# Sliding-window attention with a gated MLP on one core: other queues for the first batch, and folds of two head pairs at once in the second

## The chip, the cores and the metric

The kernel runs on one core of a Trainium2 chip. Its time is the device time of one execution in microseconds. Before the change it is 303.85 us, the median of 3 runs (303.29 to 304.75). The profiled execution took 304.4 us, of which the profile's span covers 302.7; the rest lies around it.

The engines are TensorE (PE; its weight loads are shown as PEld), VectorE (DVE), ScalarE (ACT), GpSimd (POOL) and SyncE (SP). DMA transfers are issued from SP's queue and from POOL's queue. Only the transfers that POOL issues can change the type of what they move (the casting queue).

## The reference

Eight batches of eight heads, 576 positions, 64 values per head. Each query sees itself and the 63 positions before it. The result of the attention, with the heads side by side, goes through an MLP with a gate of its own.

```python
batch, n_heads, seq, head_dim = (8, 8, 576, 64)
n_tokens, d_model, d_ff = (4608, 512, 2048)

scores = scale * np.matmul(q, k.transpose(0, 1, 3, 2))     # scale = 1/8
mask = (rel >= 0) & (rel < window)                         # window = 64
scores = np.where(mask, scores, -1000000000.0)
attn = softmax(scores)
x = np.matmul(attn, v)                # heads side by side: (4608, 512)
h = x @ w_in
g = h * np.clip(h + 3.0, 0.0, 6.0) / 6.0
out = g @ w_out
```

## The kernel before

Everything is computed in bf16 with f32 sums. The heads are taken in four pairs per batch, since a head has 64 values and a tile 128 partitions. The attention of a batch works in blocks of 64 queries: eight blocks per pair with their 128 keys each (64 before, 64 own), and the ninth block of all four pairs together, called "e".

The MLP works on tiles of 512 tokens, nine in all (`NTT`), as if the batches were one long list. For each tile, 16 chunks of the hidden layer are computed by L685 (`s1_part`, `win` against `xT`), gated by ACT (L698) and DVE (L703) into `gT`, and multiplied by `wout` (L724, `s2_part`), 64 matmuls of 512 columns per tile and direction. The attention of batch b+1 is woven into the MLP of tile b.

The order of the instructions of each engine is computed when the kernel is built. A planner (class `Plan`) holds every step with its engine, an assumed duration, what it reads and writes and a priority, and puts the steps in an order by list scheduling. Some steps may go to one of several engines (`copy_op`, `alts`), and the planner picks. The table `LANDED` gives it assumed landing times for the transfers of the first batch. What comes out is a fixed order for each engine; every engine then works through its own list and waits where its next step is not ready. The accumulators in PSUM are two banks `pn` and three double banks (`pb`, two `pa`), handed out by the planner too.

**Batch 0.** q and k must be turned so that the 64 values of a head lie along the partitions. They are loaded with nine neighbouring positions per partition (`A`, [128, 4 pairs, 9, 64]). Pair 0 comes by SP as f32 into `stage` (`load_pair`) and is cast by DVE or ACT (L343); pairs 1 to 3 come by POOL's casting queue, one transfer per pair and tensor (`load_cast`). `fold_pair` turns a pair with 18 TensorE transposes of 64x64 (L490): head h of the pair uses rows and output partitions 64h to 64h+63. One copy (L495, 576 columns) brings the result from PSUM into `F_`. `scores` first adds a far negative number to the masked places with `ident` and `far` (L514) and then multiplies (L529), two heads in turn in the two row halves.

V is wanted twice: as it lies, and shifted by 64 positions, because a block's keys begin at a multiple of 64. In batch 0, V of pairs 0 and 1 comes by SP as f32 into a second `stage` (`load_tok`, four transfers), and `cast_v` casts it straight into both places (L343, pieces on ACT and DVE). V of pairs 2 and 3 comes by the casting queue (`load_vhead`, one transfer per head), and `shift_v` copies it (L433, two copies per pair: 4 blocks and 3 blocks) on POOL, ACT or DVE. `pv_rows` multiplies (L574, columns of TensorE in halves) and normalises on DVE (L584, L585); `turn_x` turns the result (L600) into `xT`.

**Batch 1.** q and k are loaded by two `load_cast` per tensor (pairs 0, 1 and pairs 2, 3) and turned with `fold_pair` again, eight times. V comes by POOL in rows (`load_vrows`), one transfer per block, and `shift_v` copies each pair.

**Batches 2 to 7.** `load_rows` brings q and k as rows by POOL into `nq` and `nk`, and two DMA transposes on SP's queue turn them into `Tq` and `Tk`. A small POOL copy (L801, `hold`) keeps the next transfers back until `Tk` is there; then V and the rows of the following batch are issued.

POOL's queue is one list: transfers are issued in the order of the chain (`then`), each 0.5 to 0.9 us, with POOL's own copies between them where the planner puts them. Eight semaphores are used in turn for POOL's transfers, so a transfer waits until the one eight places earlier has landed.

Of the kernel before, what the change touches and what calls it, by code (L numbers as in the profile page):

```python
# [23 lines left out]
    "SP": (2970, 3660, 6210, 7840, 8150, 10350),  # L24
    "POOL": (4550, 6480, 7920, 9200, 10360, 10930, 11370, 11790, 12210, 12680),
# [187 lines left out]
def kernel(  # L213
# [41 lines left out]
    def wide(op, name):  # L255
        s, k = op.got[name]
        return banks[k][s]
# [10 lines left out]
    NST = 2  # L268
# [17 lines left out]
    def k_cols(b, r, g, j):  # L286
        k0 = max(j - 1, 0) * D
        if b < ROWS_FROM:
            return F_["k"][r, g, k0 : k0 + P]
        return T_["k"][r, g, k0 : k0 + P]  # L290
# [37 lines left out]
    def act(n):  # L328
        return 160 + n / 1.2
# [54 lines left out]
    def load_pair(n, src, b, g, i, x):  # L384
        st = stage[i][:, x * R * D : (x + 1) * R * D]
        dma(P, 106, st, src[b, 2 * g : 2 * g + 2].rearrange("h (p j) d -> (h p) (j d)", j=R), writes=[("stp", n, g)])
        copy_op(R * D, A[n][:, g, :, :].rearrange("p j d -> p (j d)"), st, ("ACT", "DVE"),
                [("stp", n, g)], [("A", n, g)] + st_keys(i, 0, NG, range(KB)), sbuf=True, prio=700)
# [5 lines left out]

    def load_tok(src, b, i, g0, g1, kbs=tuple(range(KB))):
        st = stage[i][:].rearrange("p (k h d) -> p k h d", k=KB, h=H)
        hs = slice(2 * g0, 2 * g1)
        for kb in kbs:
            s0, ss = kb * P, min(P, S - kb * P)
            dma(ss * (g1 - g0) * 2, 18, st[:ss, kb, hs, :],  # L400
                src[b, hs, s0 : s0 + ss, :].rearrange("h s d -> s h d"),
                writes=st_keys(i, g0, g1, (kb,)))

    def load_heads(src, b, i, g):

        st = stage[i][:].rearrange("p (k h d) -> p k h d", k=KB, h=H)
        for h in range(2):
            dma(NE * P, 18, st[:, 0:NE, 2 * g + h, :], src[b, 2 * g + h, 0:MAIN, :].rearrange("(k s) d -> s k d", k=NE),
                writes=st_keys(i, g, g + 1, range(NE), (h,)))
        load_tok(src, b, i, g, g + 1, (NE,))  # L410

    def st_keys(i, g0, g1, kbs, hs=(0, 1)):
        return [("st", i, g, kb, h) for g in range(g0, g1) for kb in kbs for h in hs]
# [25 lines left out]

    def cast_v(i, g0, g1, engines, prio=0, after=(), parts=((0, NE), (NE, NE)), pieces=(0, 1, 2)):  # L440
        st = stage[i][:].rearrange("p (k g h d) -> p k g h d", k=KB, g=NG, h=2)
        gs = slice(g0, g1)
        vv = V[:, :, :, 0 : 3 * D].rearrange("p k g (t d) -> p k g t d", d=D)
        full, odd = parts
        for x, (rows, src, k0, (y, n)) in enumerate((
            (slice(0, P), slice(0, P), 0, full),
            (slice(0, D), slice(D, P), 0, odd),
            (slice(D, P), slice(0, D), 1, odd),
        )):
            if not n or x not in pieces:  # L450
                continue
            blks = range(y, y + n)
            k0 += y % NE
            copy_op(n * (g1 - g0) * P, vv[rows, y : y + n, gs, 0:3:2, :], st[src, k0 : k0 + n, gs, :, :], engines[x],
                    st_keys(i, g0, g1, range(k0, k0 + n)), [("V", g, x, blk) for g in range(g0, g1) for blk in blks],
                    sbuf=True, prio=prio, after=after)
# [9 lines left out]
    def v_block(j):  # L466
        return j // 2 if j % 2 or j == 0 else NE + j // 2 - 1
# [11 lines left out]
    def fold_pair(n, g, b, gate, kinds=("n", "b", "a")):  # L479
# [19 lines left out]
        e = add("DVE", 0, None, reads=[key], writes=[t_key(n, b, g)], alts=alts, stream="copy", prio=(1400 if g == NG - 1 else 700) if b == 0 else 300)  # L499
# [3 lines left out]
    def scores(b, items, gate, stream="att", pr=300, masked=False, kinds=("a",)):  # L503
# [18 lines left out]
        def em():  # L522
            for x, name in zip(items, names):
                to = wide(add_far if masked else op, name)
                for y in range(NG if x == "e" else NM):
                    g, j = (y, NM) if x == "e" else (x, y)
                    for h in range(2):
                        r = slice(h * D, (h + 1) * D)
                        nc.tensor.matmul(to[:, h, y * D : (y + 1) * D], lhsT=k_cols(b, r, g, j),  # L529
                                         rhs=q_cols(b, r, g, j), start=not masked,  # L530
                                         stop=not masked or y == NM - 1)
# [3 lines left out]
        for x, name, key in zip(items, names, keys):  # L535
# [8 lines left out]
            def ex(name=name, n=n, p_=p_):  # L544
                nc.scalar.activation(out=p_[:].rearrange("p j h c -> p h j c"),  # L545
                                     in_=wide(add_far if masked else op, name)[:, :, 0 : n * D].rearrange("p h (j c) -> p h j c", c=D),
                                     func=EXP, scale=scale)
# [61 lines left out]
    def pv(b, x, i, after=(), stream="att", pr=300):  # L609
# [12 lines left out]
        def em():  # L622
            for h in range(2):
                for y in range(n // D):
                    g, blk, p_ = (y, 2 * NE - 1, p9[b % 2]) if end else (x, v_block(y), pT[i])
                    nc.tensor.matmul(wide(op, name)[:, h, y * D : (y + 1) * D], lhsT=V[:, blk, g, h * D : h * D + P],  # L626
                                     rhs=p_[:, y, h, :], start=True, stop=True)
# [205 lines left out]
    NOW, REST = ((0, NE), (NE, NE - 1)), ((0, 0), (2 * NE - 1, 1))  # L833
# [29 lines left out]
    for t in range(NTT):  # L863
# [24 lines left out]
        if b < B:  # L888
            if b == 1:
                gate = (hs[4],)  # L890
                cast_v(iv, 0, 2, (THREE,) * 3, parts=REST, prio=-2500, pieces=(1,))
# [66 lines left out]
```

## Time and profile before

| | |
|---|---|
| median of 3 runs | 303.85 us |
| the profiled execution | 304.4 us |
| its span | 302.7 us |
| TensorE busy | 289.8 us (96%) |
| DVE, ACT, POOL busy | 199.6, 207.5, 127.1 us |
| read from and written to HBM | 36.70 MB, 9.44 MB |
| L724, one matmul of 512 columns, start to start | 0.215 us |
| first matmul of L685 | 17.34 us |
| L685 of tile 1 begins | 55.36 us |

Times inside the span count from its start. A line of a timeline has the start, the duration, the engine, the line of the kernel, the operation, what it writes and reads, how often, and in brackets the idle time before it with what ended it. A line of the chain of waits has the start, the duration and what the end of the program was waiting for in that time; "DMA Ak<-in_k_dram" is the time from the issue of a transfer to its landing. Busy shares of TensorE contain the overlap of matmuls and say little alone: a wait shows as a gap between starts.

### The profile page before, as it was taken

How to read it: one execution, taken by the hardware profiler on the slowest of the kernel's cores; microseconds unless marked ns; L12 is line 12 of the kernel's file. 1: busy time of each engine (PE TensorE's matmuls, PEld its weight loads, DVE VectorE, ACT ScalarE, POOL GpSimd, SP SyncE). 2: the span in 40 equal slices, each digit the busy share in tenths (PEclk: the TensorE clock that was granted, in tenths of full speed). 3: DMA queues.
4: the chain of work that ended last, by engine and by line, in shares of the span. 5: the costliest groups of instructions: out<-in, count | busy, mean ns of one | idle time of the engine just before them, and what ended most of it. 6: DMA issues, size and time to landing. Idle time of an engine off the chain costs nothing.

```text
span 302.7 us, 6789 instructions
## 1 busy us (share of the span) xinstructions
PE 289.8 (96%) x2703; PEld 154.5 (51%) x2749; DVE 199.6 (66%) x326; ACT 207.5 (69%) x323; POOL 127.1 (42%) x178
## 2 busy tenths in 40 slices
PE   7799998999999999999999999999999999999996
PEld 6544554445544454445587554455445544444443
DVE  3659737686578795788777885778678767206700
ACT  4768846678778785878678767877687858217711
POOL 8874769409920990496089229803200000000000
DMA  8999999999998999999999989948900010011011
GB/s 169 194 209 205 205 185 111 109 193 89 166 115 183 99 144 151 177 128 90 204 178 120 135 162 175 128 90 163 141 2 35 36 69 3 35 69 37 0 69 69
DMA packets 137760, 36.65 MB, mean 121 GB/s; under 512 B 126337, under 2 KB 132993, under 8 KB 137729
## 3 DMA queue, kind: packets, MB, share of 16 engines
q0 software_dynamic: 98896, 17.80, 73.0%
q1 hardware_dynamic: 38832, 18.42, 24.7%
q8 instruction: 21, 0.34, 0.5%
q14 instruction: 11, 0.08, 0.1%
HBM read 36.70 MB, written 9.44 MB: 152 GB/s over the span
## 4 chain that ended last, share of the span: by engine, by line
PE 77%; DMA 10%; POOL 6%; issue 4%; DVE 1%; ACT 0%; SPq 0%; POOLq 0%; DVEq 0%
PE pn L724 33%; PE pn L685 15%; PE pa L685 12%; PE pb L685 8%; DMA Ak<-in_k_dram 7%; PE pa L626 4%; POOL nk L366 2%; DMA Tk<-nk 2%; DMA V<-in_v_dram 1%; PE pa L529 1%; POOL V L433 1%; PE pa L724 1%; POOL nq L366 1%; POOL V L366 1%; PE pb L626 1%
## 5 line engine op out<-in xcount | busy, mean ns | idle before, releaser
L724 PE MATMUL pn<-wout,gT 128*128 128x512 bf16 x532 | 125.2, 379 | 2.1 <-issue 1.1
L685 PEld LDWEIGHTS <-win 128*128 128x128 bf16 x640 | 61.9, 98 | 60.8 <-issue 0.3
L724 PEld LDWEIGHTS <-gT 128*128 128x128 bf16 x592 | 54.1, 98 | 57.5
L685 PE MATMUL pn<-xT,win 128*128 128x512 bf16 (+1 forms) x274 | 63.2, 358 | 0.4
L703 DVE SCALAR_TENSOR_TENSOR gT<-t,pn 128x512 bf16<-128x512 bf16 x63 | 43.1, 686 | 11.1 <-ACT t L698 10.9
L698 ACT ACTIVATE t<-pn,half 128x512 bf16<-128x512 f32 x63 | 43.3, 689 | 9.9 <-PE pn L685 9.4
L685 PE MATMUL pa<-xT,win 128*128 128x512 bf16 (+1 forms) x202 | 48.0, 358 | 0.3
L703 DVE SCALAR_TENSOR_TENSOR gT<-t,pa 128x512 bf16<-128x512 bf16 x47 | 32.1, 687 | 23.7 <-ACT t L698 23.4
L366 POOL DMA_DIRECT2D nk<-in_k_dram x60 | 45.9, 812 | 1.2 <-DMA Ak<-in_k_dram 0.7
L698 ACT ACTIVATE t<-pa,half 128x512 bf16<-128x512 f32 x47 | 32.1, 687 | 8.6 <-PE pa L685 8.1
L646 DVE TENSOR_TENSOR xT<-pa,rec 64x512 bf16<-64x512 f32 (+1 forms) x48 | 32.5, 677 | 6.7 <-ACT rec L635 5.7
L685 PE MATMUL pb<-xT,win 128*128 128x512 bf16 (+1 forms) x149 | 35.3, 357 | 0.5 <-issue 0.5
L366 POOL DMA_DIRECT2D V<-in_v_dram x40 | 33.2, 853 | 4.7 <-PE pa L529 1.2
L703 DVE SCALAR_TENSOR_TENSOR gT<-t,pb 128x512 bf16<-128x512 bf16 x34 | 23.3, 687 | 16.3 <-ACT t L698 16.3
L737 ACT COPY osb<-pn 128x512 f32<-128x512 f32 x18 | 10.5, 585 | 33.5 <-PE pn L724 33.5
L632 ACT ACTIVATE rec<-pa 64x512 f32<-64x512 f32 (+1 forms) x48 | 27.9, 582 | 5.2 <-PE pa L626 4.1
L801 POOL COPY scrap<-Tk 128x1 bf16<-128x1 bf16 x6 | 1.1, 188 | 69.5 <-DMA Tk<-nk 69.5
L698 ACT ACTIVATE t<-pb,half 128x512 bf16<-128x512 f32 x34 | 23.4, 689 | 7.7 <-PE pb L685 7.7
L366 POOL DMA_DIRECT2D nq<-in_q_dram x30 | 27.6, 920 | 2.4 <-DMA wout<-in_moe_w_out_dram 1.6
L545 ACT ACTIVATE pT<-pa 128x1024 bf16<-128x1024 f32 x24 | 23.6, 1020 | 0.5 <-PE pa L529 0.5
L626 PEld LDWEIGHTS <-V 128*128 128x128 bf16 x464 | 17.5, 98 | 8.8 <-DVE xT L646 1.5
L554 DVE TENSOR_TENSOR pT<-pT,mask 128x1024 bf16<-128x1024 bf16 x28 | 19.1, 698 | 4.1 <-ACT pT L545 4.0
(88 smaller groups left out, 210.0 us busy)
## 6 DMA issues: line engine op xcount, KB each, us to landing
out_dram<-osb SPq DMA_DIRECT2D x35, 256.0 KB, 2.5
V<-in_v_dram POOLq DMA_DIRECT2D x28, 128.0 KB, 4.3
nq<-in_q_dram POOLq DMA_DIRECT2D x24, 128.0 KB, 4.1
nk<-in_k_dram POOLq DMA_DIRECT2D x48, 64.0 KB, 3.9
wout<-in_moe_w_out_dram POOLq DMA_DIRECT2D x4, 512.0 KB, 14.8
win<-in_moe_w_in_dram POOLq DMA_DIRECT2D x3, 512.0 KB, 9.8
V<-in_v_dram POOLq DMA_DIRECT2D x12, 64.0 KB, 5.6
Aq<-in_q_dram POOLq DMA_DIRECT2D x2, 288.0 KB, 14.0
```

Of the source, the lines that this page charges most:

```text
L366: em = lambda: e.dma_start(out=out_ap, in_=in_ap)
L433: alts = {e: (c, (lambda e=e, rows=rows, src=src, k0=k0, n=n: cpy(e)(out=vv[rows, NE : NE + n, gs, 0:3:2, :], in_=vv[src, k0 : k0 + n, gs, ...
L545: nc.scalar.activation(out=p_[:].rearrange("p j h c -> p h j c"), in_=wide(add_far if masked else op, name)[:, :, 0 : n * D].rearrange("p ...
L554: nc.vector.tensor_tensor(out=pp, in0=pp, in1=mask[:, m0 : m0 + n, :, :].rearrange("p j h c -> p (j h c)"), op=MULT)
L626: nc.tensor.matmul(wide(op, name)[:, h, y * D : (y + 1) * D], lhsT=V[:, blk, g, h * D : h * D + P], rhs=p_[:, y, h, :], start=True, stop=True)
L632: add("ACT", act(n), lambda h=h: nc.scalar.activation(out=rc[rows[h], 0:n], in_=wide(op, name)[rows[1 - h], h, 0:n], func=LN), reads=[key] ...
L646: nc.vector.tensor_tensor(out=o, in0=a, in1=z, op=MULT)
L685: nc.tensor.matmul(bank(op, name)[:, to : to + n], lhsT=win16[:, g, fc * P : (fc + 1) * P], rhs=xT[:, g, o : o + n], start=(g == 0), stop= ...
L698: nc.scalar.activation(out=t1[ti][:], in_=bank(op, name), func=RELU, bias=half[:], scale=1.0 / 6.0)
L703: nc.vector.scalar_tensor_tensor(out=gT[:, fc, :], in0=t1[ti][:], scalar=1.0, in1=bank(op, name), op0=MIN, op1=MULT)
L724: nc.tensor.matmul(bank(op, name)[:, 0:n], lhsT=gT[:, fc, col : col + P], rhs=wout16[:, fc, js], start=(fc == 0), stop=(fc == NFC - 1))
L737: alts = {e: (f(n), (lambda e=e: cpy(e)(out=osb[oi][:, js], in_=bank(op, name)[:, 0:n])), False) for e, f in (("DVE", dve), ("ACT", act))}
```

## The change

There are three parts. The lines L626, L685, L724 and so on are those of the kernel before.

1. Batch 0: SP loads q and k of pairs 0 and 1 as f32 (four big transfers, into the one `stage` that is left). The casting queue loads q and k of pairs 2 and 3 in one transfer each, and V of all four pairs by heads (eight transfers). `load_tok`, `load_heads` and `cast_v` go; `shift_v` now copies all four pairs.
2. Batch 1: `fold_quad` turns two pairs at once: 18 transposes with all 128 rows and 128 columns, pair g in output partitions 64(g mod 2) to 64(g mod 2)+63, and one copy of 1152 columns instead of two of 576. Four such folds take the place of eight. In `F_` of batch 1 the row half is now given by the parity of the pair, not by the head.
3. The scores of batch 1 therefore alternate between two pairs, so that neighbouring matmuls use different row halves; the block "e" is stored in another order, which its exponential and `pv` follow.

The assumed landing times in `LANDED` change with the transfers. In the order that the planner makes of it, batch 1 has five shift copies of V on POOL and three on DVE (before: six and two), and all four copies out of the folds on ACT (before: four on ACT, four on DVE). From tile 1 on the order of all engines is as before.

```diff
 LANDED = {
-    "SP": (2970, 3660, 6210, 7840, 8150, 10350),
-    "POOL": (4550, 6480, 7920, 9200, 10360, 10930, 11370, 11790, 12210, 12680),
+    "SP": (2900, 3700, 5400, 7100),
+    "POOL": (7100, 8900, 9350, 9800, 10250, 10700, 11150, 11600, 12050, 12500),
 }
...
-    NST = 2
+    NST = 1
...
+    QUAD = 1
+
+    def half_rows(b, g, h):
+        x = g % 2 if b == QUAD else h
+        return slice(x * D, (x + 1) * D)
+
-    def q_cols(b, r, g, j):
+    def q_cols(b, g, h, j):
+        r = half_rows(b, g, h)
         if b < ROWS_FROM:
-            return F_["q"][r, g, j * D : (j + 1) * D]
+            return F_["q"][r, g // 2 * 2 + h if b == QUAD else g, j * D : (j + 1) * D]
...
+    def fold_quad(n, y, b, gate):
+
+        name = ("F", n, b, y)
+        key = ("ps", name)
+        gs = (2 * y, 2 * y + 1)
+        op = pe(R * 60, None, [("A", n, g) for g in gs] + ["ident"], [key], "pick", alloc=(name,), kinds=("b", "a"), after=gate, mode="c")
+
+        def flat():
+            return wide(op, name).rearrange("p x c -> p (x c)").bitcast(BF16)
+
+        def em():
+            for j in range(R):
+                for g in gs:
+                    nc.tensor.transpose(out=flat()[(g % 2) * D : (g % 2 + 1) * D, j * P : (j + 1) * P], in_=A[n][:, g, j, :], identity=ident[:])
+
+        op.emit = em
+
+        def ev(eng):
+            cpy(eng)(out=F_[n][:, 2 * y : 2 * y + 2, :].rearrange("d h (p j) -> d h p j", j=R),
+                     in_=flat()[:, 0 : R * P].rearrange("d (j h p) -> d h p j", h=2, p=D))
...
+            if b == QUAD:
+                todo = [t for pair in zip(*([t for t in todo if t[1] % 2 == x] for x in range(2))) for t in pair]
+            for name, g, h, y, j in todo:
+                u, y = (y % 2, y // 2 * 2 + h) if b == QUAD and j == NM else (h, y)
+                nc.tensor.matmul(wide(add_far if masked else op, name)[:, u, y * D : (y + 1) * D], lhsT=k_cols(b, g, h, j),
+                                 rhs=q_cols(b, g, h, j), start=not masked, stop=not masked or y == NM - 1)
...
-    i0, iv = new_stage(), new_stage()
-    load_pair("q", q, 0, 0, i0, 0)
-    load_pair("k", k, 0, 0, i0, 1)
-    load_tok(v, 0, iv, 0, 2, range(NE))
-    then(load_cast("q", q, 0, 1, 2))
-    then(load_cast("k", k, 0, 1, 2, after=chain))
+    i0 = new_stage()
+    for g in range(2):
+        load_pair("q", q, 0, g, i0, 2 * g)
+        load_pair("k", k, 0, g, i0, 2 * g + 1)
+    then(load_cast("q", q, 0, 2, 4))
+    then(load_cast("k", k, 0, 2, 4, after=chain))
     then(add("POOL", 600, lambda: make_identity(nc, ident32), writes=["c32"], after=chain))
-    then(load_cast("q", q, 0, 2, 3, after=chain))
-    then(load_cast("k", k, 0, 2, 3, after=chain))
     then(add("POOL", 900, mask_pool, writes=["m32"], after=chain))
     add("DVE", 550, far_mask, reads=["m32"], writes=["far"], prio=600)
-    then(load_cast("q", q, 0, 3, 4, after=chain))
-    then(load_cast("k", k, 0, 3, 4, after=chain))
-    for g in range(2, NG):
+    for g in range(NG):
         for h in range(2):
             then(load_vhead(0, g, h, chain)).prio = 3000
...
-    for parts in ((0, 2), (NE, 1)), ((2, 2), (NE + 1, 2)):
-        cast_v(iv, 0, 2, (THREE,) * 3, prio=700, parts=parts)
...
-    for g in range(2, NG):
+    for g in range(NG):
         shift_v(g, g + 1, THREE, 700)
...
-                for g in range(NG):
+                for y in range(NG // 2):
                     for n in "qk":
-                        fold_pair(n, g, 1, gate, ("b", "a"))
+                        fold_quad(n, y, 1, gate)
```

More of the change, by code (lines that the diff above doesn't have):

```diff
@@ L438, in shift_v @@
                 stream="copy" if len(engines) > 1 else engines[0])
[L440 to L456, printed above, removed]
     V_PARTS = [(0, blk) for blk in range(NE)] + [(x, NE + blk) for x in (1, 2) for blk in range(NE - 1)]
@@ L522, in em @@
         def em():
+            todo = []
             for x, name in zip(items, names):
-                to = wide(add_far if masked else op, name)
                 for y in range(NG if x == "e" else NM):
                     g, j = (y, NM) if x == "e" else (x, y)
[L527 to L531, printed above, removed]
+                    todo += [(name, g, h, y, j) for h in range(2)]
+            if b == QUAD:
[4 more added lines that the diff above has]
+                                 rhs=q_cols(b, g, h, j), start=not masked, stop=not masked or y == NM - 1)
         op.emit = em
@@ L542, in scores, with ex @@
                 got.append(i)
-            def ex(name=name, n=n, p_=p_):
-                nc.scalar.activation(out=p_[:].rearrange("p j h c -> p h j c"),
+            def ex(name=name, n=n, p_=p_, to="p (x y) h c -> p x (y h) c" if b == QUAD and x == "e" else "p j h c -> p h j c"):
+                nc.scalar.activation(out=p_[:].rearrange(to, **({"x": 2} if "x" in to else {})),
                                      in_=wide(add_far if masked else op, name)[:, :, 0 : n * D].rearrange("p h (j c) -> p h j c", c=D),
@@ L625, in em @@
                     g, blk, p_ = (y, 2 * NE - 1, p9[b % 2]) if end else (x, v_block(y), pT[i])
+                    at = y % 2 * 2 + y // 2 if end and b == QUAD else y
                     nc.tensor.matmul(wide(op, name)[:, h, y * D : (y + 1) * D], lhsT=V[:, blk, g, h * D : h * D + P],
-                                     rhs=p_[:, y, h, :], start=True, stop=True)
+                                     rhs=p_[:, at, h, :], start=True, stop=True)
         op.emit = em
```

31 lines of the change are left out of this document (9 added, 22 removed).

## The prediction

> **What bounds the kernel now.** I read the page first (busy shares, the slices), then the chain of waits cut into 0 to 60 us and 60 to 80 us, then the timelines of TensorE and GpSimd over batch 1.
>
> ```profile
> span 302.7 us, 6789 instructions
> PE 289.8 (96%) x2703; PEld 154.5 (51%) x2749; DVE 199.6 (66%) x326; ACT 207.5 (69%) x323; POOL 127.1 (42%) x178
> ...
> DMA  8999999999998999999999989948900010011011
> ...
> PE 77%; DMA 10%; POOL 6%; issue 4%; DVE 1%; ACT 0%; SPq 0%; POOLq 0%; DVEq 0%
> ```
>
> TensorE is the bound, but the chain leaves it for DMA and POOL in 16% of the span, and the DMA engines are full from the second slice on. So a shorter piece of TensorE work only counts where no transfer ends a wait behind it. The chain shows where those waits are:
>
> ```profile
> 5.53 6.77 DMA Ak<-in_k_dram
> ...
> 12.66 0.45 PE pn L490 x16
> ...
> 16.36 0.70 DVE opg L585
> ...
> 17.95 0.40 PE pa L600 x4
> ...
> 27.96 13.26 DMA Ak<-in_k_dram
> ...
> 46.35 1.41 POOL V L433 x2
> ```
>
> The head waits until 12.30 us for the last k of batch 0; from 18.4 us the matmuls of L685 run without a gap. Batch 1 waits for k of pairs 2 and 3, which lands at 27.96 + 13.26 = 41.22 us. Then the copies that shift V on POOL take over.
>
> ```profile
> 40.68 0.47 PE L490 MATMUL pb<-fold,Aq 64*64 64x64 bf16 x18
> ...
> 41.27 0.47 PE L490 MATMUL pa<-fold,Ak 64*64 64x64 bf16 x18
> ...
> 44.46 0.44 PE L529 MATMUL pa<-Fq,Fk 64*128 64x64 bf16 x18 [0.19 <-DVE Fk L495]
> ...
> 50.19 0.38 PE L574 MATMUL pb<-V,pT 128*64 128x65 bf16 x12 [0.83 <-POOL V L433]
> ```
>
> TensorE reaches the fold of that k at 41.27, 0.05 after it landed: work and DMA are level there. At 50.19 it has lost 0.83 to a POOL copy. POOL's own timeline and the chain after it:
>
> ```profile
> 46.35 2.08 POOL L433 COPY V<-V 64x384 bf16<-64x384 bf16 x3
> 48.38 0.76 POOL L366 DMA_DIRECT2D nk<-in_k_dram  x1
> 49.18 2.18 POOL L433 COPY V<-V 64x384 bf16<-64x384 bf16 x3
> 51.31 0.74 POOL L366 DMA_DIRECT2D nk<-in_k_dram  x1
> ```
>
> ```profile
> 62.80 4.97 DMA Tk<-nk
> ...
> 76.70 0.83 POOL V L433
> 77.58 0.58 PE pb L626 x14
> ```
>
> This is the place that decides. Six copies (4.26 us) stand between the loads of batch 2's rows; after them come the last loads, the transposes Tq and Tk (landed 67.77), the V loads on POOL, back to back from 68.43, and one V copy that ends at 77.53. TensorE had stood since 76.72 and goes on at 77.58. Whatever TensorE gains before 76.7 without POOL is lost in this wait.
>
> **The change, part by part.** *Transfers of the head.* By the DMA view of 2.5 to 3.5 us SP alone moves 0.31 MB of 2304-byte rows: a pair's 288 KB take 0.94 us. From 9.5 to 10.5 us the casting queue moves 0.19 MB: a pair's 144 KB take 0.78. From 11.75 to 12.25 us 606 small packets of V land: 512 take 0.42. From 6.5 to 8.5 us SP moves 1184 small packets and POOL 0.18 MB; 0.18 MB is 0.97 us, so 1184 packets have 1.03 and 512 take 0.45. V costs nothing either way (4 x 0.03 = 0.12 less, left as noise). q and k of pair 1 on SP cost 2 x (0.94 - 0.78) = +0.33 us.
>
> Against that stands a hole. From 3.75 to 6.0 us the queues moved 0.20 MB cast (1.36 pairs, 1.06 us), 0.03 MB of the last k row block (0.10) and some 470 small packets (0.41): 1.57 us of work in 2.25, 0.68 lost. SP has four big loads queued there afterwards, so the hole may close (-0.68), stay, or reach over the longer stretch (a rival). Effect on the transfer stream: +0.33 - 0.68 = -0.35 to +0.33; I take 0, the middle, since no row says which half of the hole was SP's.
>
> *Queues of the head.* SP issues four big loads (0.40 each) instead of two and four of 0.5, and has nothing else before 40.53: nothing. On POOL two q, k loads of 0.70 and eight V loads of 0.77, 7.6 us, stand before the loads of `win`; before it was six of 0.57 and four of 0.77, 6.5. The seventh and eighth V also wait for the landing of q and k, eight loads earlier. The first `win`, issued at 9.62, goes out at 11.0; it landed 5.8 later, behind other transfers. Now V ends at 13.0 to 13.6 (below) and 256 KB of `win` need 1.3 at the 200 GB/s of the slices: 14.9, before L685 wants it at 17. Hidden; if the issue were a further 2 us late, L685 would wait.
>
> *Compute of the head.* q and k need 4 x 0.94 + 4 x 0.78 = 6.9 us from 2.0 on, plus a hole of 0 to 0.68 and some 0.65 from last packet to landing: 9.5 to 10.2 against 12.30. V then needs 8 x 0.42 = 3.4 more: 13.0 to 13.6. Behind it come one shift copy (0.3 on DVE, 0.6 to 0.7 on POOL), the product (0.45), L584 and L585 (0.21 + 0.69), the turn (0.40) and its copy (0.58). But DVE normalises four pairs at 0.9 each, ACT has four evictions of 1.02, and the shifts now come in between: by hand the last norm starts at 16.5 against 16.97. Gain 0.45 (bounds 0 and 1.2). It ends at the landing of 41.22, so its worth is nothing there. The copies of f32 V on DVE and ACT go, the shift copies come; both lie beside these chains.
>
> *Folds.* 144 transposes of 64 columns become 72 of 128. Price before: 36 from 40.68 to 41.27, 16.5 ns each, 2.4 us in all. A group of 18 new ones costs at least 0.30 (as if 128 columns cost no more than 64), at most 18 x 57 = 1.03 (the 128-column turns of L600, four in 0.23). The column halves of L574, 16 of 65 columns in 0.38, hardly overlap (24 ns, of 27 by the 215 ns of a 512-column matmul), the row halves of L490 do. I take 0.55, halves in pairs: 4 x 0.55 = 2.2 us, 0.2 less (bounds -1.2, +1.7). At the upper bound three groups bring TensorE to 41.22's landing 0.65 late (1.1 more, 0.45 less from the head), and the last adds 0.5; the wait of 0.83 at 50.19 and the one of batch 2 take that up.
>
> The Trainium skill, "TensorEngine Tiling (Array Packing)", Restrictions, says that column tiling switches the fast weight load off. The nearest row has 16 weight loads of 128x64 for L574 in 0.33 us, 20 ns each, under a 128-column move; no run shows it hurt here, and if each load doubled to 40 ns the group would be 18 x 40 = 0.72 us, inside the bounds.
>
> The evictions: eight copies of 576 (0.64 on ACT, 0.76 on DVE) become four of 1152, all on ACT. From 0.58 for 512 and 1.02 for 1024 a copy is 0.14 + 0.86 ns each: 1.13 us. The second k group has eight L724 (8 x 0.215 = 1.72) between fold and scores: hidden with 0.6 to spare, and the 0.19 wait at 44.46 goes. DVE is free of 3.04 us and takes three shift copies instead of two.
>
> *After the landing.* Fold 0.55, 8 L724, 40 scores (0.72, the same mode and alternating halves, so no change), then L724 and V products: TensorE reaches pair 2's product at 48.4, POOL's second copy for it ends at 46.35 + 0.65 + 0.76 + 2 x 0.71 = 49.2, a wait of 0.8 as before; then 0.38, 0.25 and 0.9 as in the timeline bring L685 of tile 1 to 54.7 instead of 55.36: 0.65 less.
>
> *POOL.* In the new order five copies instead of six, one before the next issue and four after: the stretch that began at 46.35 ends 4.26 / 6 = 0.71 earlier. From there loads, transposes, V loads and the copy of 76.70 follow one another without a gap that other work ends, except between the copy of L801 and the first V load: 0.35 idle in four batches, 0.91 and 1.01 in two. Mean change taken 0.05 for that. The copy ends at 76.87, TensorE, there at 76.07, goes on at 76.93: 0.65 earlier. From tile 1 on the order on all engines is the same, so the shift stays.
>
> *Sum:* head 0, transfers 0, TensorE in batch 1 -0.65 but waiting for POOL, POOL -0.65. The profiled execution of 304.4 us (span 302.7) would take 303.75; the median of 303.85 becomes 303.2 us.
>
> **Rivals.** A, the hole closes: the stream is 0.35 earlier at 41.22, so POOL's chain gains 0.65 + 0.35 = 1.0, and the 0.27 wait for a DVE copy in batch 3 at 106.76 can go too if the 0.91 before its V loads falls to 0.35. -1.0 to -1.6: 302.85 to 302.25, 302.5 in the middle. For it: SP's rows of V start late in the hole and big loads would not. Against it: the cast packets were slow there too.
>
> B, slower: the hole is what big loads from two queues do to each other. Then all of the shared stretch, 3 x 0.94 + 3 x 0.78 = 5.2 us of work, runs at 1.57 / 2.25 = 70% and loses 2.3 instead of 0.68. With the +0.33 the stream is 1.95 late, TensorE stands at the fold of k until 43.2, POOL ends 1.95 - 0.65 = 1.3 late: 305.1 (304.5 to 305.7 with the idle time before V loads). It decides once that k lands after 41.9. Against it: full throughput from 6.0 to 8.5.
>
> C, the lock. The head then has three f32 copies on DVE early (q0, q1, k1; today two) and eight casting loads of V to issue. If each DVE copy stops POOL's descriptors, the hole grows from 0.68 to 1.02, and 0.33 + 0.34 - 0.65 is nothing: 303.85. For it: the copies at 3.72 and 5.28 lie in the hole, and the issue at 3.63 took 0.66 instead of 0.55. Against it: V issues took 0.77 with a copy at 7.70 and without. The Trainium skill, "SBUF — State Buffer", the box on DVE blocking DMA, states such a lock for f32 copies; by it C holds, and the V issues of this trace do not bear it out.
>
> **How the numbers follow.** Forecast 0.45, A 0.27, C 0.10, B 0.18. About 0.5% (1.52 us) is what a measurement of this kernel tells from no change: faster means below 302.33, slower above 305.37. Faster: half of A (0.13) and the tail of the forecast, whose median of a few runs spreads as the three before do, by 0.6 to 0.9 (0.14): 0.27. Slower: B's upper part 0.12 and 0.04 for more than it: 0.16. Same 0.57. The range goes from A's far end less part of that spread, 301.9, to the middle of B with it, 305.3; the forecast's own is 302.6 to 303.9.
>
> **What would show it.** Right: the k of pairs 2, 3 lands within 0.4 of 41.2, five POOL copies of V in batch 1, Tk at about 67.1, and TensorE still waits near 76 for POOL. Wrong: no wait there (then TensorE's own gains count), a landing beyond 41.9 (B), or fold groups over 1.03 us.

## The result and the profile after

The changed kernel takes 305.9 us (median of 22 runs, 304.01 to 308.03), the kernel before 303.78 us beside it (22 runs, 303.29 to 304.75). The ratio is 1.007, 95% interval 1.0051 to 1.0088: slower by 2.1 us. Ratios leave out executions more than 1.5% above the fastest one of their kernel, which were two of the twelve of e7 below and no others. A second series of the same two kernels gave 305.71 and 304.15 us, ratio 1.0062 (1.0041 to 1.0083). The prediction was 303.2 us.

The profiled execution of the changed kernel took 305.39 us. Its page has these lines:

```profile
span 303.7 us, 6674 instructions
...
PE 294.1 (97%) x2676; PEld 154.6 (51%) x2676; DVE 198.3 (65%) x323; ACT 209.2 (69%) x322; POOL 127.5 (42%) x177
...
PEclk9799999999999999999999999999999999999999
DMA  7999999989997999999999989958900010010011
...
PE 83%; DMA 11%; POOL 2%; DVE 2%; ACT 1%; issue 1%; POOLq 0%
```

POOL's share of the chain fell from 6 to 2%, TensorE's rose from 77 to 83%. The new line is PEclk: the second slice shows 7, that is 70 to 80% of the full clock. The chain of waits, cut to the first 60 us (start, duration, what):

```profile
4.33 8.28 DMA V<-in_v_dram
12.60 0.28 issue
12.89 1.31 POOL win L374 x2
...
17.00 10.30 DMA win<-in_moe_w_in_dram
27.30 0.28 issue
27.59 14.62 DMA Aq<-in_q_dram
```

Before, the chain went from the q, k loads of the head through TensorE's work to the last k of batch 1. Now it goes through a V load (landed 12.60), POOL's issue of `win` (12.89), the landing of the last `win` (27.30) and from there to the loads of batch 1: the transfer stream has become late as a whole. POOL's timeline shows where. Kernel before:

```profile
6.05 3.00 POOL L366 DMA_DIRECT2D V<-in_v_dram  x4
9.62 0.74 POOL L366 DMA_DIRECT2D win<-in_moe_w_in_dram  x1 [0.58 <-DMA Aq<-in_q_dram]
```

Changed kernel:

```profile
4.33 4.51 POOL L374 DMA_DIRECT2D V<-in_v_dram  x6
9.76 0.74 POOL L374 DMA_DIRECT2D V<-in_v_dram  x1 [0.93 <-DMA Aq<-in_q_dram]
11.42 0.74 POOL L374 DMA_DIRECT2D V<-in_v_dram  x1 [0.92 <-DMA Ak<-in_k_dram]
12.89 2.22 POOL L374 DMA_DIRECT2D win<-in_moe_w_in_dram  x3 [0.72 <-DMA V<-in_v_dram]
```

Six V loads of 512 packets go out in 4.51 us. The seventh and eighth wait for the landing of q and of k (eight semaphores, as the prediction says), and the first `win` then waits for the landing of a V load as well: 12.89 instead of the forecast 11.0, and 9.62 before. Of these 3.3 us, 2.0 are waits for landings (0.93, 0.92 and 0.72 against the 0.58 before), the other 1.3 POOL's longer list of issues. What the DMA engines did meanwhile is in the table by stretches from 8.5 to 18 us (span of the stretch, busy time of PE, PEld, DVE, ACT, POOL, then granted clock, mean DMA occupancy, GB/s). Kernel before:

```profile
8.50:12.00 3.50, 2.59 (x89) 1.74 (x88) 2.00 (x4) 2.47 (x4) 2.54 (x4) 1.00 1.55 191
12.00:15.00 3.00, 2.38 (x79) 1.73 (x71) 2.12 (x5) 2.56 (x4) 2.55 (x5) 1.00 1.69 186
15.00:18.00 3.00, 2.44 (x47) 1.51 (x48) 2.83 (x8) 2.57 (x5) 2.96 (x6) 1.00 1.28 207
```

Changed kernel:

```profile
8.50:12.00 3.50, 2.59 (x74) 1.96 (x74) 2.36 (x4) 1.28 (x2) 1.66 (x3) 0.67 1.95 175
12.00:15.00 3.00, 3.00 (x74) 1.75 (x72) 2.16 (x6) 1.86 (x3) 2.28 (x4) 0.81 1.17 87
15.00:18.00 3.00, 2.47 (x86) 1.87 (x84) 2.10 (x6) 2.67 (x4) 2.90 (x6) 1.00 1.27 154
```

From 12 to 15 us only 87 GB/s moved instead of 186: 0.30 MB less, by an estimate 1.5 us at the 200 GB/s of the later slices. The stretches beside it lack 0.06 and 0.16 MB, another 1.1 us. TensorE has its own trouble in the same stretch, as its timeline shows:

```profile
9.17 0.47 PE L460 MATMUL pb<-fold,Aq 64*64 64x64 bf16 x18 [2.21 <-DVE Aq L351]
...
10.81 0.69 PE L460 MATMUL pn<-fold,Ak 64*64 64x64 bf16 x18 [0.24 <-DVE Ak L351]
...
18.90 0.40 PE L598 MATMUL pa<-ident,opg 128*128 128x128 bf16 x4 [0.44 <-DVE opg L583]
```

The fold of q of pair 1 starts after 2.21 us of idle time, because that q, now on SP's queue, landed at 8.49 instead of 6.44. After this gap the granted clock is 0.67. In batch 1:

```profile
42.24 0.69 PE L486 MATMUL pb<-ident,Aq 128*64 128x128 bf16 x18 [0.27 <-DMA Aq<-in_q_dram]
...
43.84 0.69 PE L486 MATMUL pa<-ident,Ak 128*64 128x128 bf16 x18
...
49.12 0.58 PE L625 MATMUL pa<-pT,V 128*128 128x64 bf16 x14 [1.03 <-DVE V L421]
```

The folds of two pairs (18 in 0.62 to 0.70 us) are near their forecast, but q and k land at 42.20 and 43.66 instead of 39.80 and 41.23, V of batch 1 correspondingly, and TensorE waits 1.03 us at 49.12 for a V copy.

The marks of eleven profiles, in us from the span's start (the columns of q, `win` and k are landings of transfers; "MLP" and "tile 3" are the first matmuls of tiles 0 and 3):

| kernel | q pair 1 | first `win` | MLP | k of batch 1 | tile 1 | tile 3 |
|---|---|---|---|---|---|---|
| before | 6.44 | 15.23 | 17.34 | 41.23 | 55.36 | 119.30 |
| changed | 8.49 | 18.34 | 19.13 | 43.66 | 57.65 | 120.19 |
| changed, again | 8.03 | 16.43 | 18.63 | 43.07 | 57.52 | 120.06 |
| e1 head alone | 9.20 | 19.88 | 20.32 | 45.39 | 59.01 | 122.33 |
| e2 folds alone | 5.97 | 15.72 | 17.87 | 41.71 | 54.55 | 119.95 |
| e3 V by POOL alone | 5.10 | 17.71 | 17.76 | 44.02 | 56.46 | 120.68 |
| e18 pair 1 by SP alone | 7.97 | 16.40 | 19.26 | 42.83 | 55.94 | 119.34 |
| e8 `win` early | 7.96 | 14.19 | 19.05 | 41.07 | 57.39 | 121.51 |
| e5 V in four loads | 8.48 | 15.16 | 21.53 | 41.10 | 59.19 | 121.59 |
| e11 V in four loads | 6.39 | 14.49 | 17.66 | 39.91 | 55.15 | 117.83 |
| e14 both cures | 5.26 | 15.73 | 18.88 | 41.04 | 55.82 | 119.35 |

From the start of tile 3 to the end of the span every kernel takes 183.4 to 183.8 us, so whatever a change does is done by then. The 2.3 us lost at tile 1 are 0.9 at tile 3: TensorE came so late that the waits of the kernel before in batches 2 and 3 (0.67 and 0.27) are gone, which is 0.9 of the 1.4 us. (The profile of before, 304.4, is one of its slower runs: the two profiled spans differ by 1.0 us, the medians by 2.1, and no trace shows the difference between the two.)

### The profile page after: what moved, and what is told of

It is laid out like the page before. It is cut to its first block, busy times and chain, and to the rows that moved or that the text cites. A ratio compares the mean times of both kernels' runs of the same rounds, so it can differ in the third digit from the quotient of the medians.

```text
span 303.7 us, 6674 instructions
## 1 busy us (share of the span) xinstructions
PE 294.1 (97%) x2676; PEld 154.6 (51%) x2676; DVE 198.3 (65%) x323; ACT 209.2 (69%) x322; POOL 127.5 (42%) x177
## 4 chain that ended last, share of the span: by engine, by line
PE 83%; DMA 11%; POOL 2%; DVE 2%; ACT 1%; issue 1%; POOLq 0%
PE pn L723 37%; PE pn L684 16%; PE pa L684 12%; PE pb L684 9%; DMA Aq<-in_q_dram 5%; PE pa L625 4%; DMA win<-in_moe_w_in_dram 3%; DMA V<-in_v_dram 3%; PE pa L528 2%; PE pa L723 1%; POOL win L374 1%; PE pb L625 1%; ACT pT L543 1%; DVE pT L552 1%; DVE opg L583 0%
## 5 line engine op out<-in xcount | busy, mean ns | idle before, releaser
L723 PE MATMUL pn<-wout,gT 128*128 128x512 bf16 x560 | 129.7, 379 | 0.0
L684 PE MATMUL pa<-xT,win 128*128 128x512 bf16 (+1 forms) x204 | 47.3, 358 | 0.0
L702 DVE SCALAR_TENSOR_TENSOR gT<-t,pa 128x512 bf16<-128x512 bf16 x46 | 31.4, 686 | 21.8 <-ACT t L697 21.5
L645 DVE TENSOR_TENSOR xT<-pa,rec 64x512 bf16<-64x512 f32 (+1 forms) x52 | 34.2, 657 | 10.7 <-ACT rec L634 9.7
L374 POOL DMA_DIRECT2D V<-in_v_dram x44 | 36.2, 841 | 5.6 <-DMA wout<-in_moe_w_out_dram 1.2
L684 PE MATMUL pb<-xT,win 128*128 128x512 bf16 (+1 forms) x156 | 37.1, 357 | 0.0
L697 ACT ACTIVATE t<-pa,half 128x512 bf16<-128x512 f32 x46 | 31.4, 687 | 7.7 <-PE pa L684 7.2
L702 DVE SCALAR_TENSOR_TENSOR gT<-t,pb 128x512 bf16<-128x512 bf16 x35 | 24.0, 686 | 18.2 <-ACT t L697 18.2
L631 ACT ACTIVATE rec<-pa 64x512 f32<-64x512 f32 (+1 forms) x52 | 29.5, 567 | 7.0 <-PE pa L625 5.9
L697 ACT ACTIVATE t<-pb,half 128x512 bf16<-128x512 f32 x35 | 24.1, 689 | 8.6 <-PE pb L684 8.6
L543 ACT ACTIVATE pT<-pa 128x1024 bf16<-128x1024 f32 x25 | 24.7, 1023 | 2.2 <-PE pa L528 2.2
```

Of the source, the lines that this page charges most:

```text
L374: em = lambda: e.dma_start(out=out_ap, in_=in_ap)
L543: nc.scalar.activation(out=p_[:].rearrange(to, **({"x": 2} if "x" in to else {})), in_=wide(add_far if masked else op, name)[:, :, 0 : n * ...
L631: add("ACT", act(n), lambda h=h: nc.scalar.activation(out=rc[rows[h], 0:n], in_=wide(op, name)[rows[1 - h], h, 0:n], func=LN), reads=[key] ...
L645: nc.vector.tensor_tensor(out=o, in0=a, in1=z, op=MULT)
L684: nc.tensor.matmul(bank(op, name)[:, to : to + n], lhsT=win16[:, g, fc * P : (fc + 1) * P], rhs=xT[:, g, o : o + n], start=(g == 0), stop= ...
L697: nc.scalar.activation(out=t1[ti][:], in_=bank(op, name), func=RELU, bias=half[:], scale=1.0 / 6.0)
```

## Experiments

The theories are named in the expectations. Each median stands beside the kernel before on the same chip.

**The parts apart.** e1 has only part 1 (the head), e2 only parts 2 and 3, each the diff above without the other part.

> Only the first part of the change: batch 0 as in the changed kernel, batch 1 with the eight old folds and the old scores. Theory H (all of the loss comes from the head: the k of pairs 2, 3 of batch 0 and the first win land late, the whole transfer stream is some 2.4 us behind, and nothing in batch 1 costs anything): 305.5 to 306.5 us, first L685 near 19, the k of batch 1 near 43.5. Theory Q (the folds of two pairs, their 1152-column copies on ACT and the later V copies cost the time): 303.5 to 304.2, as before.

> Only the second and third part: batch 0 as before, batch 1 with four folds of two pairs and scores that alternate between pairs. Theory H: 303.0 to 303.8, that is the same or up to 0.7 us less, with a group of 18 transposes at 0.55 to 0.65 us. Theory Q: 305 or more.

e1: 307.38 us, ratio 1.0103 (1.0076 to 1.0129). e2: 303.25 us, ratio 0.9968 (0.9952 to 0.9984). The head costs 3.1 us, more than theory H had (305.5 to 306.5; its profile has MLP at 20.32 and k at 45.39, not 19 and 43.5), and the folds gain. In the profile of e2, the slowest of its 12 executions (305.04), tile 1 starts 0.81 earlier than before although its head was 0.5 later, and then two waits take it back, as the prediction said of TensorE's own gains:

```profile
68.97 0.64 PE L566 MATMUL pa<-Tq,Tk 64*128 64x64 bf16 x32 [1.31 <-DMA Tk<-nk]
...
78.80 0.58 PE L663 MATMUL pb<-pT,V 128*128 128x64 bf16 x14 [1.32 <-POOL V L441]
```

The same kernel again, and the changed kernel beside it:

> The kernel with only the folds of two pairs and the alternating scores again, as it is: 302.9 to 303.6, below the kernel before by 0.5 to 1.3.

> The changed kernel again, as it is: 305.4 to 306.4. If the two queues share the engines by chance, q of pair 1 lands at another time than 8.49 in this profile (6.4 to 10.3, as in the kernels with the same first issues); if by rule, within 0.2 of it.

303.85 us, ratio 0.9988 (0.9972 to 1.0005), above what was expected: over both series the folds gain 0.1 to 0.3%. In this second profile tile 1 starts at 54.80 and the wait for POOL is there again, the one for Tk is not:

```profile
77.47 0.58 PE L663 MATMUL pb<-pT,V 128*128 128x64 bf16 x14 [1.12 <-POOL V L441]
```

The changed kernel again: 305.71. Its q of pair 1 landed at 8.03, not 8.49.

**The two halves of the head.** e3 loads V by POOL in eight loads and leaves q and k as before; e4 moves only q and k of pair 1:

```diff
-    load_tok(v, 0, iv, 0, 2, range(NE))      # e3
-    for g in range(2, NG):
+    for g in range(NG):
         for h in range(2):
             then(load_vhead(0, g, h, chain)).prio = 3000
...
+    load_pair("q", q, 0, 1, i0, 2)           # e4
+    load_pair("k", k, 0, 1, i0, 3)
-    then(load_cast("q", q, 0, 1, 2))
-    then(load_cast("k", k, 0, 1, 2, after=chain))
```

> Of the head only V: all of V by the casting queue in eight transfers, q and k as in the kernel before (pair 0 by SP, pairs 1 to 3 by the casting queue, one transfer each), batch 1 as before. If the loss of the head is the queue of small V transfers in front of win and the eight semaphores that hold win back: 305 to 306, win landing at 17 or later. If it is the big f32 loads of SP beside the casting queue: within 0.5 us of before (303.3 to 304.3).

> Of the head only q and k of pair 1: both by SP as f32, pairs 2 and 3 by the casting queue in one transfer each, V half by SP and half by the casting queue as before, batch 1 as before. If the big loads of two queues beside each other are the loss: 305 to 306, k of the last pair of batch 0 landing a microsecond or more later than 12.3. If the order of V and win on the casting queue is: within 0.5 us of before.

e3: 305.97 us, ratio 1.0057 (1.0036 to 1.0078); e4: 306.56 us, 1.0075 (1.0046 to 1.0105). In e3 TensorE's head is nearly on time (MLP at 17.76), `win` goes out at 12.18 and k of batch 1 lands 2.8 late: this is the stream alone. No landing is waited for here; the eight issues by themselves make `win` late:

```profile
6.31 5.96 POOL L366 DMA_DIRECT2D V<-in_v_dram  x8
12.18 2.31 POOL L366 DMA_DIRECT2D win<-in_moe_w_in_dram  x3
```

e4 looked as bad and missed both of its readings (the last k of batch 0 landed at 11.52, not late), but its tile 1 starts at 55.44, as before. Its loss lies later, in POOL's batch 2 and the wait that follows in batch 3:

```profile
75.12 3.29 POOL L433 COPY V<-V 64x768 bf16<-64x768 bf16 x3
```

```profile
108.75 0.58 PE L626 MATMUL pa<-pT,V 128*128 128x64 bf16 x14 [1.93 <-DVE V L433]
```

The planner had given POOL three V copies there (3.29 us) where the kernel before has one (0.82). The row loads behind them, the transposes and the V of batch 3 come 2.0 us later. e18 is e4 with these copies held to the engines of the kernel before:

```diff
-                    shift_v(g, g + 2, THREE if b == 2 else ("DVE",))
+                    shift_v(g, g + 2, {1: ("ACT",) if g else ("DVE",), 2: ("DVE",) if g else ("POOL",)} if b == 2 else ("DVE",))
```

> The kernel with only q and k of pair 1 moved to SP, and batch 2's shift copies of V held to the engines that have them in the kernel before (GpSimd one, not three). Theory G (GpSimd's two more copies delay the row loads behind them, and so the V of batch 3, by 2.5 us): the wait of 1.93 at 108.75 goes below 0.5, time 304.0 to 304.9, not told from before; pair 1 on SP costs little while win is issued as early as before. Theory P (pair 1 on SP costs by itself): 305.5 to 306.6 as with the copies on GpSimd.

304.52 us, ratio 1.0022 (1.0001 to 1.0043), and no wait at 109: pair 1 on SP by itself costs some 0.2%, V by POOL 0.57%. With the folds' 0.1 to 0.3% off, this makes 0.5 to 0.7%, against the 0.6 to 0.7% of the change; the head alone (e1) cost 1.0%, with 0.8 to 1.3 as its interval. Pair 1 on SP can make the stream late too: k of batch 1 landed at 42.83 in e18 and at 41.91 in e4, with V loaded as before.

**The stream cured.** e11 loads V in four loads of 1024 packets (`load_vrows`) instead of eight of 512; e5 is the same with the shift copies of batch 0 on DVE and ACT alone; e8 issues two loads of `win` as one behind the V of pair 0; e19 is e8 with batch 2's copies held as in e18 (e8 too had 3.29 us of them on POOL).

```diff
-    for g in range(NG):                      # e5, e11
-        for h in range(2):
-            then(load_vhead(0, g, h, chain)).prio = 3000
+    for blk in range(NE):
+        then(load_vrows(0, blk, chain)).prio = 3000
...
             then(load_vhead(0, g, h, chain)).prio = 3000
+        if g == 0:                           # e8
+            then(load_win(0, 4, after=chain)).prio = 3000
```

> The changed kernel, but V of batch 0 comes in four loads of 1024 small packets instead of eight of 512, and its shift copies run on DVE and ACT alone. Theory N (GpSimd's issue of small loads, 0.73 us each against 0.42 of transfer, starves the transfer queues and holds the loads of win back): four issues of some 0.9 instead of eight, win issued at about 10 instead of 12.9, the last k of batch 1 lands at 41.5 to 42.3 instead of 43.66, time 304.2 to 305.0. Theory S (the big f32 loads beside the casting queue are what costs, whatever V does): win may go out earlier but k of batch 1 lands within 0.5 of 43.66, time 305.5 to 306.2.

> The changed kernel, but the first two loads of win (as one of 512 KB) are issued right behind the V loads of pair 0, ahead of the other six. Theory N: large packets fill the queues while GpSimd issues the small loads, the nearly empty stretch at 12 to 15 us goes, k of batch 1 lands at 41.7 to 42.5; V of pair 3 lands up to 1.5 later than 14.97, so the first matmul of the expert stage comes at 19 to 20; time 304.3 to 305.2. Theory S: the landing stays within 0.5 of 43.66, time 305.6 to 306.5.

> The changed kernel with V of batch 0 in four loads of 1024 small packets, GpSimd still taking its share of the shift copies. Theory W (two delays of about 2 us that cover each other: the stream, and TensorE's own head, late because q and k of pair 1 land 2 us later on SP): k of batch 1 lands at 41.0 to 41.5, but the first matmul of the expert stage stays at 18.8 or later and tile 1 starts at 57 to 57.8, time 304.6 to 305.6. Theory N (the stream alone): tile 1 at 55.5 to 56.3, time 303.4 to 304.4.

> The changed kernel with two loads of win ahead of six of V, and batch 2's shift copies of V held to one on GpSimd. Theory G: no wait over 0.5 near 109, time 305.0 to 306.2, that is what TensorE's late head leaves (first matmul of the expert stage at 19) with k of batch 1 landing at 41.1. If something else in it costs: 307 or more as before.

e5 304.94 us, 1.0036 (1.0009 to 1.0062); e8 307.87, 1.0127 (1.0088 to 1.0166); e11 305.09, 1.0023 (0.9998 to 1.0048); e19 306.05, 1.0078 (1.0049 to 1.0108). In all four k of batch 1 lands at 39.91 to 41.75, against 43.07 and 43.66 in the changed kernel (in e10 below, which is e11 with a filler on TensorE, at 42.48): that the small loads ahead of `win` on POOL make the stream late is shown. The cures shorten the issues and the waits for landings at once, so they do not tell the two apart. An issue of 1024 packets took 0.89 us, one of 512 took 0.75. e8 missed its range, most likely for the reason of e4: without the copies e19 is where it was expected, though the two intervals overlap. But the time comes back by only 0.8 to 1.4 us in e5 and e11 (by the ratios, against both series of the changed kernel), and not at all in e19, because TensorE's head is late as well. In e19 the MLP begins at 20.95. In e5 and e11 four loads by rows have all to land before any product, and in e5 this shows as

```profile
18.71 0.35 PE L572 MATMUL pa<-V,pT 128*64 128x65 bf16 x11 [1.21 <-ACT V L421]
```

The two delays cover each other. e3 shows the stream's alone; e5, where the MLP begins at 21.53 with the landing as before, shows TensorE's alone, with a granted clock of 0.50 from 12 to 15 us in it. e11's profile does not show theory W: it is the fastest of 13 executions (303.02), with MLP at 17.66 and tile 1 at 55.15; only the median of 305.09 lies in that theory's range.

**The clock.** e7 and e10 put 28 matmuls on constants into TensorE's gap, in the changed kernel and in e11:

```diff
+            if op.alloc == (("F", "q", 0, 1),):
+                for _ in range(28):
+                    warm(op)
             op.emit()
```

> The changed kernel with 28 matmuls of 96 columns on constants put on TensorE ahead of the fold of q of pair 1, in the gap from 6.8 to 9.2 us. Theory K (the lowered clock after the gap costs): granted clock 1.00 in 7.6 to 15.2 us, first matmul of the expert stage at about 18.0 instead of 19.1; if the head's computing sets the end, the time falls by 0.7 to 1.1. Theory H (the landing of batch 1's k sets it): that landing stays at 43.5 to 43.8, the start of tile 1 within 0.3 of 57.65, time within 0.4 of the changed kernel's 305.9.

> The kernel with V in four loads of 1024 and, in the gap before the fold of q of pair 1, 28 matmuls of 96 columns on constants that keep TensorE's clock up. Theory W: granted clock 1.00 up to 22.8 us, expert stage from 18.2 to 18.8, landing at 41.0 to 41.5, tile 1 at 56.0 to 56.8; time 0.5 to 1.2 below the same kernel without the filler. Theory O (the clock is a sign of the gap and costs nothing): within 0.4 of the kernel without the filler.

e7: 306.86 us, ratio 1.0075 (1.0044 to 1.0106); e10: 305.78, 1.0055 (1.0029 to 1.008). In e7's profile the clock is 1.00 throughout and the MLP begins 0.75 earlier, at 18.38; the time does not fall, since TensorE then waits for the landings (k of batch 1 at 43.92):

```profile
34.19 0.69 PE L486 MATMUL pa<-ident,Aq 128*64 128x128 bf16 x18 [0.94 <-DMA Aq<-in_q_dram]
```

In e10 q of pair 1 came at 10.34, and the filler (1.36 us) covered a third of the gap: no clean test. So theory K falls for the changed kernel, whose ratio of 1.007 e7 repeats; what a low clock costs where the stream is on time stays open.

**Casting loads later, and pair 1 back.** e13 issues the casting loads of pairs 2 and 3 behind the identity and the mask; e14 is that with V in four loads; e15 has pair 1 back on the casting queue, one pair a load, and V in four loads.

```diff
-    then(load_cast("q", q, 0, 2, 4))
-    then(load_cast("k", k, 0, 2, 4, after=chain))
     then(add("POOL", 600, lambda: make_identity(nc, ident32), writes=["c32"], after=chain))
     then(add("POOL", 900, mask_pool, writes=["m32"], after=chain))
+    then(load_cast("q", q, 0, 2, 4, after=chain))
+    then(load_cast("k", k, 0, 2, 4, after=chain))
```

> The changed kernel, its order on TensorE kept, but GpSimd makes the identity and the mask first and issues the casting loads of q and k of pairs 2 and 3 behind them, some 2 us later. If the loads of pair 1 on SP are late because the casting loads share the engines with them: q and k of pair 1 land by 6.5 and 7.5 instead of 8.5 and 10.0, TensorE's gap of 2.4 falls below 1.0, the first matmul of the expert stage comes at 17.3 to 18.2; the loads of win stay late (V still issued in eight), so k of batch 1 stays at 43 to 44 and time at 305 to 306. If SP's loads are slow by themselves, q of pair 1 stays beyond 7.5 and the time rises by 1 or more.

> The kernel with both cures: casting loads of q and k of pairs 2 and 3 behind the identity and the mask, and V of batch 0 in four loads of 1024. Theory W: TensorE's head at 17.3 to 18.2, k of batch 1 at 41.0 to 42.0, tile 1 at 54.6 to 55.6, time 302.7 to 303.7, as low as with the folds alone (303.25). Theory N: no better than the kernel with the rows alone. If something else in the head costs: 304.5 or more with both landings early.

> The changed kernel with q and k of pair 1 back on the casting queue, one pair a load as before, and V of batch 0 in four loads of 1024 by the casting queue. If pair 1 on SP is the rest of the cost: q of pair 1 lands at 5.5 to 6.5, no gap over 1.2 on TensorE before 10 us, granted clock 1.00, k of batch 1 lands at 40.7 to 41.7, tile 1 at 54 to 55, time 302.8 to 303.6. If V by the casting queue costs even in four loads: products of V late (all four blocks have to land), expert stage from 18.5 or later, time 304.2 to 305.2.

e13 305.12 us, 1.0035 (1.0014 to 1.0056); e14 304.61, 1.0021 (1.0001 to 1.0042); e15 305.61, 1.0057 (1.0034 to 1.0079). e13 brought q of pair 1 to 6.95, earlier though not by 6.5, and left the stream late (k at 43.16) with the time in its range; the MLP began at 18.41, not by 18.2. e14 missed its 302.7 to 303.7 and lies in the range of "something else in the head": with pair 1 early, TensorE's wait moved to q of pairs 2 and 3 and to the V copies:

```profile
8.68 0.69 PE L460 MATMUL pa<-fold,Aq 64*64 64x64 bf16 x18 [1.56 <-DMA Aq<-in_q_dram]
...
15.46 0.87 PE L572 MATMUL pa<-V,pT 128*64 128x65 bf16 x27 [0.83 <-POOL V L421]
```

e15 lies above both of its ranges. With pair 1 where it was before, V in four loads is still late; in its profile, the slowest of its six executions, the MLP began at 19.91 and the products had waited for a V copy:

```profile
15.81 1.00 PE L572 MATMUL pa<-V,pT 128*64 128x65 bf16 x27 [1.64 <-POOL V L421]
```

So V of the first pairs by the casting queue costs either way, as far as e3 and e15 show: in eight loads by POOL's issues, in four because the first product waits for the last load.

**POOL's copies in batch 1 left out.** e6 is e2 with `shift_v(g, g + 1, ("DVE", "ACT"))` in batch 1.

> The kernel with only the folds of two pairs and the alternating scores (head as before), and with batch 1's shift copies of V on DVE and ACT alone. Theory P (GpSimd's five copies in batch 1 delay the loads behind them and so set the end of the waits in batch 2): GpSimd's chain ends 3.5 us earlier, the waits of 1.7 and 1.5 at 69 and 79 us shrink below 0.5, time 301.8 to 302.5 against 303.25. Theory D (the copies only change place: DVE and ACT get eight of 0.3 to 0.5 in a stretch where TensorE waits for them): a wait of over 1 us for DVE or ACT near 49, time 303.0 to 304.0.

303.03 us, 0.9968 (0.995 to 0.9985). The wait for POOL is gone, a new one of 0.83 us for DVE's gating step (`gT`) stands at 69.77, and the profiled run took 302.24. The wait for Tk is absent too, but of the two profiles of e2's kernel only one had it. And the ratio is that of e2's first series: what theory P says of the wait for POOL holds, its gain is not shown. The kernel of e2 and e6 are the only ones below the one before.

## Why the prediction was wrong

*Queues of the head*: this step failed. It counted 7.6 us of POOL's work and called the late `win` "Hidden; if the issue were a further 2 us late, L685 would wait". The issue was 1.9 us later than forecast (12.89), since each landing it waited for was later too and 0.72 to 0.93 us of idle time stand before each of the last three issues; the wait of `win` for a V load was not in the step at all. And L685 was not what to ask: what is late next is the stream behind `win`, the k of batch 1, which the prediction itself had found level with TensorE's work. POOL's issue took 0.75 us (six in 4.51) for a load whose transfer it had priced at 0.42: in e3, with no wait for landings, the issue and not the transfer is the limit; in the changed kernel the waits add 2.57 us to it. The Trainium skill, "DMA: Bandwidth & Descriptors", "Anatomy of one DMA", calls descriptor generation small and variable. For these loads the time of the issue on POOL, 0.75 us, is larger than the 0.42 of the transfer; the trace does not say how much of it is descriptors.

*Transfers of the head*, "I take 0": +2.43 us at the landing, of which e3 (2.8 without the f32 loads of pair 1) gives most to V. The middle, 0, was the wrong choice as well: the f32 loads beside the casting loads make the stream late too, by an amount that changes from execution to execution. Nine profiles have the same first six loads of q and k issued at the same times within 0.02 us (changed, again, e1, e5, e7, e8, e10, e11, e19); q of pair 1 landed at 8.49, 8.03, 9.20, 8.48, 8.23, 7.96, 10.34, 6.39 and 9.04. The execution of e11 with 6.39 is the only one of its 13 with a granted clock of 1.0 and took 303.02 us; the others took 304.72 to 305.97.

*Compute of the head*: the gain of 0.45 became a loss of 1.79. The step timed the k of pairs 2 and 3 (11.14, not 9.5 to 10.2) and never when pair 1 lands, which is wanted first. Of the 1.79, e7 with the clock at 1.00 has 0.75 less, with q of pair 1 landing 0.26 earlier.

*Folds*: right in kind. From the start of a group to the next instruction the four groups took 0.62 to 0.70 us each (0.55 forecast), 2.58 in all, and the eight old ones 2.86 without idle time: 0.28 less, 0.2 forecast. The groups lie between 0.55 and the 0.72 that the prediction works out for doubled weight loads. By the Trainium skill, "TensorEngine Tiling (Array Packing)", Restrictions, column tiling switches the fast weight load off; these runs neither show nor refute that. The ACT copy took 1.12 of the 1.13 forecast.

*POOL*: five copies, and in e2 the wait for POOL that takes TensorE's gain back (1.32 and 1.12 us in its two profiles), as forecast: -0.3 to -0.9 us against -0.65. In the changed kernel this step had no say, since POOL's first copy came at 48.31 and TensorE was later still.

*Rival B* gave 305.1 (304.5 to 305.7) and a landing beyond 41.9. The landing came so, the time a little above (305.9, and 305.71 in the second series), and its mechanism made part of it. It wanted 2.3 us lost in the stretch that the big loads of two queues share. The DMA view of the changed kernel for 4.0 to 8.5 us (packets, MB, share of the engines) has

```profile
q0 software_dynamic: 370, 0.41, 66.6%
q1 hardware_dynamic: 248, 0.50, 33.8%
```

which by the prediction's prices is 0.41/0.144 x 0.78 + 0.50/0.288 x 0.94 = 3.85 us of work in 4.5: 0.65 lost, no more than in the hole before. But these prices are not the least that the loads can take. In e11, with the same six loads issued at the same times, the same window has

```profile
q0 software_dynamic: 651, 0.59, 79.5%
q1 hardware_dynamic: 293, 0.59, 38.4%
```

which the same prices would make 5.1 us of work, and the last of the six landed at 8.89 us instead of 11.14; over the nine profiles it lies between 8.89 and 12.45. The stream behind pays for much of that. In the three kernels that have V in four loads behind the same six, the two landings (last of the six, k of batch 1) are 8.89 and 39.91 in e11, 10.44 and 41.10 in e5, 12.45 and 42.48 in e10. The rest is V: with the six landed at 10.74, the second profile of the changed kernel has k of batch 1 at 43.07, 2.0 later than e5. Why the six loads take so different a time stays open. Rival A's closed hole happened in one execution. Rival C: V issues took no longer than before.

## What to carry over

Before moving loads to a queue that an engine issues itself, compare the issue time with the transfer time of each load, and list the landings that each issue has to wait for; where the issue is longer or a landing is late, everything behind it on that queue is late and the DMA engines run short of work. Ask of a load what is first wanted of it and what stands behind it in the same queue up to the next point where transfers and work are level, not only whether its own reader waits. When a planner makes the order, compare the later batches too before blaming the part that was edited (e4 and e8).

## What the runs showed of the hardware

In the changed kernel a gap of 2.21 us on TensorE lies before a mean granted clock of 0.67 from 8.5 to 12 us. From 7.6 to 15.2 us the clock was 0.78 in e13, whose longest gap in the head was 0.99 us, and in the second profile of the changed kernel, with 1.13; e2 kept 1.00 with one of 1.12. The Trainium skill, "TensorE: Matmul & The Clock Gate", Part 1, gives an idle window of about 3.4 us, free-running; here a lowered clock followed much shorter gaps, and not always.

How two queues share the DMA engines differs between executions: one load, issued at 1.73 to 1.74 us in nine profiles and behind the same loads, landed between 6.39 and 10.34.
